# Memory attention and a top-1 expert layer on one core: the first batch reordered up to the choice of its expert, and a new table of places

## The chip, the core and the metric

The kernel runs on one core of one Trainium2 chip. The metric is the device time of one execution in microseconds (us). The core has five engines that each work through their own queue of instructions in order: PE (matmul; its weight loads are shown apart, as PEld), DVE (vector), ACT (scalar), POOL (general) and SP, which here issues every DMA. The engines wait for each other by semaphores. Sixteen DMA engines move data between HBM and the on-chip memory.

## What is computed

Eight batches, each with 8 heads, 576 tokens and head dimension 64. A softmax of `phi` over the tokens folds keys and values into 32 memory slots for each head; queries attend to these slots; each token's result (512 wide) goes to one of 8 experts, and the expert is chosen by token 0 and then kept or renewed token by token.

```python
a = phi - np.max(phi, axis=2, keepdims=True)
a = np.exp(a)
a = a / (np.sum(a, axis=2, keepdims=True) + 1e-09)
k_m = np.einsum('bhsm,bhsd->bhmd', a, k)
v_m = np.einsum('bhsm,bhsd->bhmd', a, v)
scores = scale * np.matmul(q, k_m.transpose(0, 1, 3, 2))
attn = softmax(scores)
x = np.matmul(attn, v_m)
logits = np.einsum('bsd,de->bse', x, w_gate)
fresh_e = int(np.argmax(logits[b, s]))
e = fresh_e if s == 0 or local_gate[b, s] < 0.5 else prev_e
h = np.maximum(x[b, s] @ w1[e], 0.0)
out[b, s] = p[e] * (h @ w2[e])
```

## The kernel before

**What runs for a batch.** For each batch there is, in this order: the softmax of phi (`colmax` the maximum over tokens, `pm`, `mc`, `pm2`, `cx` its way over partitions, `sub`, `exp`, `asum` the sum over tokens); `pkv`, 72 pairs of matmuls over nine groups of tokens that fold keys and values (tile `pkv`, L402); `sums` (L413), which brings the sums over tokens into the same PSUM tile; `rinv` and `kvn` (the division); `pT`, `kvT` (the turned form) and `pgg`, `ggt` (gate weights folded with the values). The attention is done in two parts of tokens, a (or p) and z: `qT` (queries turned on DVE), `psc` (scores, L513), `turn`, `mx`, `sub`, `exp`, `sum`, `inv`, `mul`, `at` (weights, L561), and `ah`, `al`, which split them into a high and a low half. `at store` writes them to DRAM.

**The choice.** `pl0` (L584) gives the eight logits of token 0 in tile `pl`. `c_choice` turns them on DVE into the expert's index `ei`; `expert` loads it into a register of SP; `w1 0`, `w1 1`, `w2 0`, `w2 1` then load that expert's weights into tiles `raw` (L761, L771).

**The expert.** `pg` and `G` fold w1 with the values (tiles `Gh`, `Gl`, high and low halves; L793, L805). The hidden layer (L825) runs in four chunks of 256 tokens and eight of 320, each with a PSUM tile `ph` of three in turn, which ACT and then DVE (tile `h`, L833 and L835) must empty. The second layer (tile `po`; L863 to L865 for the first tokens, L913 to L915 for the turned rest) uses w2 split into `w2h` (ACT, L782) and `w2l` (POOL, L783).

**What sets the order.** Everything is put into the engines' queues in the order in which the program is written. `start()` writes out by hand all work of batch 0 up to its first hidden chunk, mixed with the softmax of phi of batch 1. After it the generator `moe(b)` issues the hidden and the second layer of batch b and yields a modelled time after each chunk; the table `PLACES` gives for each step of each batch the modelled time (37.8 a batch) at which it is issued between these chunks. A step placed later stands behind more chunks in every queue that it uses. On SP, which also works in order, a load whose buffer isn't free yet holds up all loads behind it: behind w1 of batch 0 stand v of batch 1, w2, the next queries `q_t` (L253), phi, w2's second half, keys and values, and the store of `at`.

**Warm matmuls.** `warm(n)` issues n matmuls on zeros (tile `wp`, L305, 128 x 512) with no use for the result.

After the eight batches a loop over listed (batch, expert) pairs recomputes the tokens that left the expert of token 0; with these inputs it has no iteration.

## Time and profile before

| | |
|---|---|
| runs | 414.0, 413.4, 411.82 us; median 413.4 |
| the profiled execution | 414.21 us, its span 412.4 us |
| granted PE clock | 0.998 |
| PE busy | 391.7 us (95%), PEld 327.3 (79%) |
| DVE busy | 284.2 us (69%) |
| ACT, POOL busy | 179.4 us (44%), 151.3 us (37%) |
| DMA | 82.59 MB, mean 200 GB/s |

The span is what the profile's times are counted in; the profiled execution's own time is 1.8 us longer. PE stands still for 412.4 - 391.7 = 20.7 us in all, about 6 of them in the tail, where the last outputs are stored. Rows of a timeline read: start, length, engine, line, operation, out<-in, size, count, and in brackets the idle time before and what ended it. Rows of the chain read: start, length, engine or DMA, line. SPq is SP's work of issuing a DMA.

### The profile page before, as it was taken

The numbers are of one execution on the slowest core, as the hardware profiler recorded it, in microseconds if no ns is written. First come the engines' busy times: TensorE is split into PE (matmuls) and PEld (weight loads), VectorE is DVE, ScalarE is ACT, GpSimd is POOL, SyncE is SP. The second block draws the span as 40 slices with busy tenths as digits, with TensorE's granted clock in tenths as the row PEclk, the third lists the DMA queues.
The fourth block names the chain that finished last, engine by engine and source line by source line (L and its number), as shares of the span: only waits on it lengthen the run. The fifth ranks groups of instructions, "written<-read, shape, count | busy, mean of one in ns | idle before, by whom it ended". The sixth has DMA issues, their size and how long they took to land.

```text
span 412.4 us, 10572 instructions
## 1 busy us (share of the span) xinstructions
PE 391.7 (95%) x4170; PEld 327.3 (79%) x4174; DVE 284.2 (69%) x714; ACT 179.4 (44%) x434; POOL 151.3 (37%) x162
## 2 busy tenths in 40 slices
PE   8787888999999989999999999999999999999994
PEld 2546867898788967798878997799888996999883
DVE  5486797868977798697769777787767674736300
ACT  2153652446553744335542464445531563255010
POOL 3024451437341844029510691029400671065000
PEclk9999999999999999999999999999999999999999
DMA  8969792999297939699979197956784177002011
GB/s 238 328 201 269 139 396 95 232 255 383 61 357 160 369 106 241 140 351 351 263 169 399 28 282 146 338 227 175 159 209 170 31 238 288 28 0 65 25 39 57
DMA packets 115446, 82.59 MB, mean 200 GB/s; under 512 B 69616, under 2 KB 89088, under 8 KB 115392
## 3 DMA queue, kind: packets, MB, share of 16 engines
q1 hardware_dynamic: 115328, 81.84, 66.9%
q8 instruction: 35, 0.57, 0.6%
q0 software_dynamic: 64, 0.02, 0.2%
q14 instruction: 19, 0.16, 0.1%
HBM read 66.60 MB, written 15.24 MB: 198 GB/s over the span
## 4 chain that ended last, share of the span: by engine, by line
PE 68%; DMA 11%; SPq 11%; DVE 6%; issue 2%; ACT 1%; DVEq 0%; ACTq 0%
PE ph L825 19%; SPq L253 7%; PE po L863 7%; PE po L913 7%; PE po L865 6%; PE po L864 6%; PE po L915 6%; PE po L914 6%; DMA att_d<-at 6%; PE pkv L402 3%; PE pg L793 3%; DMA raw<-in_moe_w_dram 3%; DMA kv_t<-in_v_dram 2%; PE psc L513 2%; DVE h L835 1%
## 5 line engine op out<-in xcount | busy, mean ns | idle before, releaser
L783 POOL TENSOR_TENSOR w2l<-raw,w2h 128x512 fp32r<-128x512 f32 x64 | 82.4, 1312 | 29.3 <-ACT w2h L782 22.9
L825 PE MATMUL ph<-ah,Gh 128*128 128x256 f32 (+1 forms) x256 | 74.1, 304 | 2.1 <-DVE h L835 1.3
L835 DVE SCALAR_TENSOR_TENSOR h<-ph,h 128x320 fp32r<-128x320 f32 (+2 forms) x104 | 52.7, 519 | 32.2 <-ACT h L833 31.6
L825 PE MATMUL ph<-ah,Gl 128*128 128x256 f32 (+1 forms) x256 | 72.0, 296 | 0.1
L913 PE MATMUL po<-h,w2l 128*128 128x320 f32 x224 | 71.4, 319 | 0.0
L915 PE MATMUL po<-h,w2h 128*128 128x320 f32 x224 | 69.2, 309 | 0.0
L914 PE MATMUL po<-h,w2h 128*128 128x320 f32 x224 | 69.1, 309 | 0.0
L833 ACT ACTIVATE h<-ph 128x320 fp32r<-128x320 f32 (+1 forms) x96 | 46.4, 489 | 40.5 <-PE ph L825 40.2
L920 POOL TENSOR_TENSOR oT<-oT,gT 128x320 f32<-128x320 f32 x28 | 20.8, 742 | 107.5 <-DVE oT L919 93.7
L863 PE MATMUL po<-w2h,h 128*128 128x512 f32 (+1 forms) x152 | 60.0, 395 | 0.0
L864 PE MATMUL po<-w2l,h 128*128 128x512 f32 (+1 forms) x152 | 57.8, 380 | 0.5 <-POOL w2l L783 0.5
L865 PE MATMUL po<-w2h,h 128*128 128x512 f32 (+1 forms) x152 | 57.7, 380 | 0.0
L825 PE MATMUL ph<-al,Gh 128*128 128x256 f32 (+1 forms) x256 | 55.2, 296 | 0.5 <-issue 0.4
L825 PEld LDWEIGHTS ph<-ah,Gh 128*128 128x128 f32 x256 | 48.1, 188 | 7.4 <-DVE h L835 3.4
L825 PEld LDWEIGHTS ph<-ah,Gl 128*128 128x128 f32 x256 | 48.2, 188 | 0.5 <-DVE Gl L805 0.4
L913 PEld LDWEIGHTS po<-h,w2l 128*128 128x128 f32 x224 | 42.0, 188 | 5.0 <-issue 4.5
L569 POOL TENSOR_TENSOR al<-at,ah 128x576 fp32r<-128x576 f32 (+1 forms) x18 | 23.1, 1291 | 62.3 <-ACT ah L565 49.5
L782 ACT ACTIVATE w2h<-raw 128x512 fp32r<-128x512 f32 x64 | 38.4, 624 | 11.8 <-PE po L915 8.9
L914 PEld LDWEIGHTS po<-h,w2h 128*128 128x128 f32 x224 | 42.1, 188 | 0.2
L915 PEld LDWEIGHTS po<-h,w2h 128*128 128x128 f32 x224 | 42.1, 188 | 0.0
L825 PEld LDWEIGHTS ph<-al,Gh 128*128 128x128 f32 x256 | 41.2, 188 | 0.9 <-issue 0.6
L863 PEld LDWEIGHTS po<-w2h,h 128*128 128x128 f32 x152 | 28.6, 188 | 11.6 <-issue 7.0
(156 smaller groups left out, 581.4 us busy)
## 6 DMA issues: line engine op xcount, KB each, us to landing
raw<-in_moe_w_dram SPq DMA_DIRECT2D x34, 512.0 KB, 5.9
raw<-in_moe_w_dram SPq DMA_DIRECT2D x15, 1024.0 KB, 5.7
kv_t<-in_k_dram SPq DMA_DIRECT2D x7, 1152.0 KB, 10.0
kv_t<-in_v_dram SPq DMA_DIRECT2D x7, 1152.0 KB, 12.2
q_t<-in_q_dram SPq DMA_DIRECT2D x112, 72.0 KB, 3.4
att_d<-at SPq DMA_DIRECT2D x8, 576.0 KB, 7.6
out_dram<-oT SPq DMA_DIRECT2D x28, 160.0 KB, 5.8
out_dram<-ot SPq DMA_DIRECT2D x17, 256.0 KB, 5.4
```

Source lines behind the costliest of these rows:

```text
L253: nc.sync.dma_start(out=st.qt[p0 : p0 + 32, h], in_=qv[h, g, j])
L782: nc.scalar.activation(h, src, AF.Copy)
L783: nc.gpsimd.tensor_tensor(out=l, in0=src, in1=h, op=ALU.subtract)
L825: nc.tensor.matmul(pv[:, c - c0], lhsT=lt[:, g, cs], rhs=rt[:, g, s0 : s0 + n], start=(i == 0), stop=(i == 5),)
L833: nc.scalar.activation(hc[:, :, 0:n], pv, AF.Relu)
L835: nc.vector.scalar_tensor_tensor(out=hc[:, :, o : o + z - a], in0=pv[:, :, a:z], scalar=0.0, in1=hc[:, :, a:z], op0=ALU.max, op1=ALU.subtract,
L863: nc.tensor.matmul(po[:, c0:c1], lhsT=h[:, c, th], rhs=hi, start=(c == 0), stop=False)
L864: nc.tensor.matmul(po[:, c0:c1], lhsT=h[:, c, th], rhs=lo, start=False, stop=False)
L865: nc.tensor.matmul(po[:, c0:c1], lhsT=h[:, c, tl], rhs=hi, start=False, stop=(c == FC - 1))
L913: nc.tensor.matmul(po[:, 0:n], lhsT=lo, rhs=h[:, c, 0:n], start=(c == 0), stop=False)
L914: nc.tensor.matmul(po[:, 0:n], lhsT=hi, rhs=h[:, c, 0:n], start=False, stop=False)
L915: nc.tensor.matmul(po[:, 0:n], lhsT=hi, rhs=h[:, c, n : 2 * n], start=False, stop=(c == FC - 1))
```

## The change

The table of places gets new numbers. Keys and values are folded in two steps ("pkv 0" five groups of tokens, "pkv 1" four), the loads of queries are two steps ("q 0", "q 1"), and qT has two buffers. For batch 0 the sums come from one product with a block matrix of ones, in a PSUM tile of their own, ahead of the second piece of pkv, with rinv directly behind. The choice uses MAX and MAX_INDEX, and the index is loaded into SP's register without the two instructions that assert its bounds. `start()` is written in another order: 66 warm matmuls of 32 columns and 8 wide ones stand in place of 11 wide ones; the transposes of the larger part's queries stand ahead of `pl`, and nothing else; the choice stands ahead of `pm` of batch 1; the split of `at` into halves is done for each head group; exp and asum of batch 1 move out of `start()` into the table. In the first batch's loop "pg 1" and "pkv 0" stand between the first two hidden chunks. The scores of part z of batches 1 and 2 use PSUM tiles of the hidden layer, and `w_pg` takes another PSUM pool for the last batch's second half.

```diff
-    "pkv": {1: 1.52, 2: 34.49, 3: 70.3, 4: 93.6, 5: 127.71, 6: 165.81, 7: 204.5},
+    "pkv 0": {1: 0.14, 2: 30.71, 3: 66.71, 4: 92.5, 5: 127.8, 6: 165.6, 7: 203.7},
+    "pkv 1": {1: 1.86, 2: 32.7, 3: 66.71, 4: 94.32, 5: 127.8, 6: 165.6, 7: 203.7},
...
     def f_sums(st):
+        if st.b == 0:
+            st.sums = ps_a.tile([P, NG], F32, tag="pa", name="sums")
+            nc.tensor.matmul(st.sums, lhsT=st.asum.rearrange("p h m -> p (h m)"), rhs=ones, start=True, stop=True)
+            return
...
     def c_choice(st):
         pl = st.pl0
-        l0 = pga.tile([1, E], F32, tag="l0", name="l0")
-        m0 = pga.tile([1, 1], F32, tag="m0", name="m0")
+        m8 = pga.tile([1, 8], F32, tag="m8", name="m8")
         c0 = c0s[st.b % 2]
-        nc.vector.tensor_reduce(out=m0, in_=pl[0:1, 0:E], axis=AX.X, op=ALU.max)
-        nc.vector.scalar_tensor_tensor(
-            out=l0, in0=pl[0:1, 0:E], scalar=m0, in1=code[0:1], op0=ALU.is_equal, op1=ALU.mult
+        st.ei = pga.tile([1, 8], mybir.dt.uint32, tag="ei", name="ei", bufs=3)
+        nc.vector.max(out=m8, in_=pl[0:1, 0:E])
+        nc.vector.max_index(out=st.ei, in_max=m8, in_values=pl[0:1, 0:E])
+        nc.vector.tensor_scalar(
+            out=c0[0:1], in0=st.ei[:, 0:1], scalar1=-1.0, scalar2=float(E), op0=ALU.mult, op1=ALU.add
         )
-        nc.vector.tensor_reduce(out=c0[0:1], in_=l0, axis=AX.X, op=ALU.max)
-        st.ei = pga.tile([1, 1], I32, tag="ei", name="ei", bufs=3)
-        nc.vector.tensor_scalar(out=st.ei, in0=c0[0:1], scalar1=-1.0, scalar2=float(E), op0=ALU.mult, op1=ALU.add)
...
-        st.e = nc.sync.value_load(st.ei[0:1, 0:1], min_val=0, max_val=E - 1)
+        st.e = nc.values_load(
+            st.ei[0:1, 0:1],
+            engines=(mybir.EngineType.SP,),
+            min_val=0,
+            max_val=E - 1,
+            skip_runtime_bounds_check_because="an index of the gate's E values",
+        )
...
-        warm(11)
+        warm(66, 32)
+        warm(8)
...
-        warm(14)
+        warm(12)
...
         for i in range(2):
             f_asum_piece(s, i)
-            f_pkv(s, PIECES[i])
-            warm(3 * (1 - i))
+        f_pkv(s, PIECES[0])
         f_sums(s)
+        f_rinv(s)
+        warm(3)
+        f_pkv(s, PIECES[1])
         fetch_kv(n, (0,))
+        f_kvn(s)
         k_q0(s, EARLY[0])
-        f_rinv(s)
-        f_kvn(s)
+        f_pT(s)
+        warm(2)
+        f_kvT(s)
         f_colmax_tree(n, slice(0, 1))
-        warm(4)
-        f_pT(s)
-        warm(3)
-        f_kvT(s)
-        f_colmax_tree(n, slice(1, 4))
...
-        for f in steps:
+        for f in steps[:4]:
             f(s, EARLY[0])
-        p, z = EARLY[1:]
+        f_colmax_tree(n, slice(1, 2))
         k_q0(s, p)
-        f_pm(n)
-        warm(3)
-        f_mc(n)
+        for f in steps[4:]:
+            f(s, EARLY[0])
         c_pl(s)
+        f_colmax_tree(n, slice(2, 4))
         c_choice(s)
         expert(s)
```

On PE, at the start of batch 0, from the first pkv to the logits of token 0 (pq: transposed queries, wp: warm matmuls, of which only one of each stretch is shown). Before:

```order
L402 MATMUL pkv<-kv_t,phi_t 32x128 x48
...
L402 MATMUL pkv<-kv_t,phi_t 32x128 x24
L413 MATMUL pkv<-ones,asum 32x1 x8
L499 MATMUL pq<-ident,q0e 128x32 x4
...
L441 MATMUL pT<-ident,kvn 128x128 x2
...
L513 MATMUL psc<-qT,kvT 32x32 x8
L459 MATMUL pgg<-wg,kvT 32x9 x8
L502 MATMUL pq<-ident,q_147 64x128 x16
L346 MATMUL pm<-ident,cm 128x128
...
L584 MATMUL pl_399<-ggt_108,at 1x8 x2
```

The change, at the same place:

```order
L407 MATMUL pkv<-kv_t,phi_t 32x128 x48
L418 MATMUL sums<-ones,asum 128x2
...
L407 MATMUL pkv<-kv_t,phi_t 32x128 x24
L510 MATMUL pq<-ident,q0e 128x32 x4
L452 MATMUL pT<-ident,kvn 128x128 x2
...
L526 MATMUL psc<-qT,kvT 32x32 x8
L470 MATMUL pgg<-wg,kvT 32x9 x8
L513 MATMUL pq<-ident,q_149 64x128 x16
L597 MATMUL pl_439<-ggt_110,at 1x8 x2
L351 MATMUL pm<-ident,cm 128x128
```

The sums moved ahead of the second piece of pkv, pm of batch 1 moved behind pl, and pl stands directly behind the 16 transposes. Ahead of the first pkv stand 26 warm matmuls before and 87 in the change.

On PE, in batch 0's hidden layer, from the end of the first chunk to the third (pg: w1's second half folded with the values; pkv: batch 1's; only the first row of a chunk is shown). Before:

```order
L793 MATMUL pg<-raw_421,kvT 32x512 x8
L825 MATMUL ph<-ah,Gh 128x256
...
L402 MATMUL pkv<-kv_t,phi_t 32x128 x72
L413 MATMUL pkv<-ones,asum 32x1 x8
L825 MATMUL ph<-ah,Gh 128x256
```

The change:

```order
L805 MATMUL pg<-raw_455,kvT 32x512 x8
L407 MATMUL pkv<-kv_t,phi_t 32x128 x40
L838 MATMUL ph<-ah,Gh 128x256
...
L407 MATMUL pkv<-kv_t,phi_t 32x128 x32
L422 MATMUL pkv<-ones,asum 32x1 x8
L838 MATMUL ph<-ah,Gh 128x256
```

40 of the 72 pairs moved ahead of the second chunk; the other 32 and the sums stay between the second and the third.

On DVE, in batch 2's hidden layer, around the column maximum of batch 4 (cm; sc: scores of the attention; qT: turned queries; h: hidden chunks of 256 and then 320 tokens). Before:

```order
L835 SCALAR_TENSOR_TENSOR h_2152<-ph,h_2152 128x2x256
L486 STREAM_TRANSPOSE qT<-q_t 128x576
L835 SCALAR_TENSOR_TENSOR h_2152<-ph,h_2152 128x2x256
L310 TENSOR_REDUCE cm<-phi_t 128x128
L835 SCALAR_TENSOR_TENSOR h_2255<-ph,h_2255 128x320
L549 TENSOR_REDUCE sm<-sc 128x18
```

The change:

```order
L848 SCALAR_TENSOR_TENSOR h_2183<-ph,h_2183 128x2x256
L315 TENSOR_REDUCE cm<-phi_t 128x128
L848 SCALAR_TENSOR_TENSOR h_2183<-ph,h_2183 128x2x256
L848 SCALAR_TENSOR_TENSOR h_2284<-ph,h_2284 128x320
L562 TENSOR_REDUCE sm<-sc 128x18
```

The column maximum moved ahead of the last chunk of 256 tokens, and a transpose of queries left this stretch. Elsewhere, `pl` of batch 1 stands behind 14 po rows of three matmuls in the change and behind 12 before, and pl of batch 6 moved from the end of batch 4's second layer into batch 5's hidden layer.

## The prediction

> **What bounds the kernel now.** I read the busy shares first, then the busy time stage by stage, then PE's waits, then the chain of work that ended last. The stages (start, rest of batch 0, then 46 us for each batch) show where PE has anything left to win. The first number behind the window is its length, the second PE's busy time; the last three are PE's granted clock, the DMA share and GB/s:

> ```profile
> 0.00:29.61 29.61, 23.13 (x380) 12.65 (x384) 17.35 (x46) 10.10 (x23) 4.73 (x30) 1.00 0.84 252
> 29.61:80.00 50.39, 44.73 (x495) 35.99 (x488) 39.79 (x93) 22.91 (x57) 22.83 (x28) 1.00 0.84 236
> 80.00:126.00 46.00, 46.00 (x503) 39.18 (x502) 38.88 (x107) 23.84 (x60) 19.35 (x16) 1.00 0.82 245
> 126.00:172.00 46.00, 44.67 (x654) 35.46 (x652) 37.25 (x90) 23.37 (x57) 19.10 (x15) 1.00 0.74 206
> ```

> PE is idle 29.61 - 23.13 = 6.48 us before the first hidden matmul of batch 0 and 50.39 - 44.73 = 5.66 us in the rest of that batch, then 0 and 1.33 us in two whole batches, at a full clock. From 80 us on the kernel is PE's own work in PE's own order. A new table of places that keeps this work can only take idle time away, so the change is worth what it does in the first 80 us and to a few single waits later. Idle time ahead of 29 us counts only where it lies on the chain that ends in the chosen expert's weights. That chain (start, length, what):

> ```profile
> 11.14 1.58 PE pkv L402 x95
> ...
> 17.00 1.39 issue
> ...
> 18.79 1.90 PE pq L502 x32
> ...
> 21.60 0.19 PE pl L584 x4
> ...
> 21.81 0.17 DVE m L597
> ...
> 22.57 0.14 DVE ei L603
> ...
> 23.27 0.18 SPq L1046
> ...
> 23.75 0.41 SPq L761
> ...
> 51.29 12.46 DMA att_d<-at
> ```

> The load of v ends, then pkv, psc and the transposes of the queries (pq) follow; the logits of token 0 (pl) choose the expert, and at 23.75 SP issues the load of w1. Behind it SP issues v of batch 1, w2, the next queries, the next keys and values and the store of at, so everything that the DMAs carry from 24 to 64 us hangs on 23.75.

> **The start, part by part.**

> ```profile
> 1.19 4.21 PE L305 MATMUL wp<-wz 128*128 128x512 bf16 x11 [1.19 <-DVE wz L163]
> L305 PEld LDWEIGHTS <-wz 128*128 128x128 bf16 x43 | 4.3, 109 | 6.9 <-issue 3.5 <-DVE wz L163 1.2
> 10.79 0.29 DVE L393 TENSOR_TENSOR asum<-asum,tree 128x128 f32<-128x128 f32 x1
> 15.11 0.37 ACT L433 ACTIVATE kvn<-pkv,rinv 128x128 f32<-128x128 f32 x1
> ```

> The sums of batch 0 become one matmul ahead of the second piece of pkv, and rinv follows while PE works on. So kvn, which began at 15.11 behind pkv, sums and rinv, starts straight behind pkv, which ended near 14.4: 0.7 us earlier, 0.5 with seams. Of the warm matmuls behind it, two go from in front of pT and one from behind it.

> The 66 small warm matmuls ahead of everything have no row. A pkv pair takes 1.58 / 95 = 0.017 us, and a weight load of a warm matmul 0.109, so all take between 1.1 and 7.2 us. I take 0.05 each, 3.3 us, since their 32 columns stand nearer to pkv. With the eight wide ones (8/11 of 4.21 = 3.1) the first pm is issued at 7.6, where the eleven ended at 5.4. What hides it is v, on which pkv waits until 11.14: asum ended at 11.08 and sums need it only when pkv 0 is through, at 12.7. asum 2.2 us later, at 13.3, would hold sums for 0.6; but from here to the gate there are 1.4 us of slack, as follows. I take 0. At 7.2 us asum would come at 17.2 and the slack would be gone.

> The 1.39 us "issue" stall stands inside psc, among matmuls of one kind with their inputs there.

> ```profile
> 0.00:17.10 17.10, 13.79 (x218) 6.90 (x221) 8.16 (x19) 3.69 (x7) 3.47 (x28) 1.00 0.95 273
> 17.10:41.80 24.70, 19.16 (x379) 13.42 (x380) 17.29 (x43) 11.89 (x27) 7.97 (x10) 1.00 0.81 243
> ```

> From this stall to the next one of its kind (42.07, quoted below) lie 379 matmuls and 380 weight loads, 759 instructions, near to three times 256: I read both as instructions that are loaded by the block and came late while the DMAs were full. Ahead of the first pkv now stand 61 more warm matmuls with their weight loads (87 against 26), 122 instructions, so both this boundary and the one a block before it come earlier: the one before moves out of pkv into the warm matmuls that run while v is awaited, and the next block is asked for some microseconds sooner. So the stall leaves the chain. [...]

> Then PE meets the queries. The larger part's transposes now stand ahead of pl. Their loads, by issue and landing:

> ```profile
> L291 SPq DMA_DIRECT2D q<-in_q_dram x2: 1574/2163/2752, 6.8 to 9.5; - x2
> DMA to landing us min/median/max: 8.8/8.9/9.1
> ```

> The second is issued at 9.5 and lands 8.8 later, at 18.3. The transposes take the two head groups in turn, one from each load, so the 1.9 us cannot run before, and pl comes at 20.3 to 20.45. I take 20.45, against 21.60: 1.15 us. Upstream, 0.5 and 1.39 make 1.9; the softmax of the small part, about 2.5 us on DVE, then ends near 19, ahead of pl by 1.4. That is the slack: what is won upstream beyond it is lost here.

> The choice takes 0.90 us from m to the end of ei (21.81 to 22.71). MAX and MAX_INDEX have no row: four operations with their gaps make 0.90, so two make 0.45, and 1.0 if the index costs three. I take 0.5: 0.4 us won. SP's assert instructions behind the register load (from 23.27 to just ahead of 23.58) go: 0.26. So w1 is issued 1.15 + 0.4 + 0.26 = 1.8 us earlier, at 21.95. The ends: -1.7 (sums at 17.2 in place of 12.7, so pl 3.1 later, and the dear index 0.5) and 2.1 (pl at 20.3, an index as cheap as m).

> How much of this lead reaches PE is decided further on:

> ```profile
> 33.03 1.09 PE L793 MATMUL pg<-raw,kvT 64*32 64x512 f32 x16 [0.97 <-DMA raw<-in_moe_w_dram]
> 36.05 2.25 PE L402 MATMUL pkv<-kv_t,phi_t 64*32 64x128 f32 x144 [0.31 <-DMA kv_t<-in_v_dram]
> 39.12 0.39 PE L825 MATMUL ph<-ah,Gh 128*128 128x256 f32 x1 [0.78 <-DVE Gl L805]
> 42.07 0.39 PE L825 MATMUL ph<-al,Gh 128*128 128x256 f32 x1 [0.43 <-issue]
> ```

> Before: chunk 0, pg 1, chunk 1, pkv, sums, chunk 2 (39.12). Now pkv 0, five of nine tokens, stands between pg 1 and chunk 1, and queued behind it are chunk 1, pkv 1, sums and chunk 2, with ACT and DVE waiting for their results. pkv 0 needs v, which landed at 36.0; 1.8 us earlier that is 34.2, while pg 1 is through at 34.12 - 1.8 = 32.3. So PE idles 1.9 us there, then runs pkv 0 (5/9 of 2.25 = 1.25), chunk 1 (36.05 - 0.31 - 34.12 = 1.6), pkv 1 (1.0) and sums (0.25): chunk 2 at 34.2 + 4.1 = 38.3, a gain of 0.8, which is SP's lead less 1.0. Gl's 0.78 lies under the new order, as G 1 has some 5 us. Of the 0.43 I count 0.3, since its block boundary moves too. Start together: **-1.1**.

> **The places.**

> ```profile
> 60.12 0.50 PE L864 MATMUL po<-w2l,h 128*128 128x512 f32 x1 [0.46 <-POOL w2l L783]
> 64.80 0.24 PE L584 MATMUL pl<-ggt,at 128*1 128x8 f32 x4 [1.20 <-DVE at L561]
> 276.99 0.24 PE L584 MATMUL pl<-ggt,at 128*1 128x8 f32 x4 [0.59 <-DVE at L561]
> 55.11 0.69 PE L513 MATMUL psc<-qT,kvT 64*32 64x288 f32 x8 [0.59 <-DVE qT L486]
> ```

> pl of batch 1 moves behind six more po matmuls (some 1.4 us of work), which cover its 1.20, and the cause, the store of at (51.29, 12.46 us), goes out earlier with all that is ahead of it on SP: **-1.2**, at worst 0. pl of batch 6 moves by several chunks: **-0.6**. w2's second load has SP's lead of 1.8 against PE's of 1.1: **-0.3** of 0.46. psc of batch 1 waits for qT, which now stands behind one more h on DVE (0.48 below): **+0.4**.

> The fourth wait is 1.33 us. The column maximum of batch 4's phi sits on DVE between two h, and PE needs the h behind it to free one of three buffers:

> ```profile
> 141.52 0.69 DVE L835 SCALAR_TENSOR_TENSOR h<-ph,h 128x512 fp32r<-128x512 f32 x1
> 143.56 2.24 DVE L310 TENSOR_REDUCE cm<-phi_t 128x128 f32<-128x1152 f32 x1
> 145.72 0.48 DVE L835 SCALAR_TENSOR_TENSOR h<-ph,h 128x320 fp32r<-128x320 f32 x1
> 146.25 0.41 PE L825 MATMUL ph<-ah,Gh 128*128 128x320 f32 x1 [1.33 <-DVE h L835]
> ```

> It moves ahead by one h. Then it runs from 142.2 to 144.4, the h behind it (0.69) ends near 145.05, and that one frees the buffer of the chunk one earlier, which was due 0.9 us ahead of the stalled one (146.25 - 1.33 - 0.9, about 143.95): a wait of 1.1. The 2.24 us are moved, not hidden: **-0.2**, though -1.33 if DVE is early for another reason.

> New waits: some hundred entries moved, and the whole batches above had between none and 1.33 us. I allow one of the middle size, **+0.6**. The second query buffer, pkv in two pieces and pg 1 in another pool add no work; I cost them at nothing, hidden under PE's own work as the full stage above is, and at one wait of 1.3 if that cover is gone.

> Sum: -1.1 - 1.2 - 0.6 - 0.3 + 0.4 - 0.2 + 0.6 = -2.4 us. The profiled execution took 414.2 (span 412.4), 0.8 above the median of 413.4 and at the top of 411.8 to 414.0. The sum gives 411.8 against 414.2 and 411.0 against the median; I predict 411.0.

> **Rivals.** *The gains are absorbed*: pkv 0 eats the lead, the store of at lands when it did (12.46 us in a stage with a DMA share of 0.84), and PE waits as before, somewhere else. Only -0.6 and -0.3 stay: 413.3, or 412.5 from the median. For it: both first stages are full on DMA. *All targeted waits go*: a lead of 2.1 (-1.1 and -0.43), then 1.2, 0.59, 0.46, 0.59 and 1.33, and no new wait: -5.7, so 408.5, or 407.7 from the median. Against it: qT behind one more h, and the 2.24 us that only move. *On the other side, the small warm matmuls hold up asum*, the gate, and with it v, and pkv 0 stands ahead of chunk 1. Slower from where the lead is under 1.0: pl past 21.25, sums past 14.9, asum 3.8 late, which is 0.075 us for each of the 66. At 0.109, pl is 3.1 later, the lead 1.85 - 3.1 = -1.25, and chunk 2 comes 2.25 later; w2's saving is lost: 414.2 + 2.25 - 1.2 - 0.6 + 0.4 + 0.6 = 415.65, and 416.15 with the dear index. Against it: pkv's narrow products at 0.017. *The change doesn't do what it says*: the stall comes back between pkv and pl. It costs up to 1.39, as much as the slack there, so the forecast stands.

> **How the numbers follow.** A measurement of this kernel tells about 0.5%, 2.07 us, from no change: the bounds are 411.3 and 415.5. The forecast (409.5 to 412.3) has 0.50, six parts in ten of it below 411.3. Absorbed: 0.22. All waits gone: 0.18. Slower by the warm matmuls: 0.10, most of it past 415.5. Faster is 0.30 + 0.18 and a little of the absorbed, 0.51; slower 0.08; the same 0.41. The range takes in the absorbed case, the forecast and most of "all waits gone", and stops short of the slower case: 407.4 to 414.8.

> **What would show it.** Right: w1 issued near 22.0; no issue stall between pkv and pl; pl at 20.4 straight behind the transposes; a new wait of PE for v of 1.5 to 2 us ahead of pkv 0; chunk 2 near 38.3; no wait of pl for at in batches 1 and 6; a wait of about 1 us left at the column maximum of batch 4. Wrong: a lead of SP under 1.0, sums waiting for asum, or waits of over 0.6 us in batches that had none.

## The result and the profile after

The change takes 415.8 us (median of nine runs, 414.17 to 417.8) against 412.63 (nine runs of the kernel before, 411.63 to 414.14). The ratio is 1.0078, with a 95% interval of 1.0052 to 1.0103: slower by 0.8%, where 411.0 was predicted and 414.8 was the end of the range. The profiled execution took 415.16 us (span 413.4, PE clock 0.986). The profiled execution of before that the prediction used was a long one: a second profile of the same kernel (e8 below) took 412.15, and its 2.0 us lie behind the third hidden chunk of batch 0, half of them ahead of batch 1. One execution of e4, of 954 us, is left out of every time below.

The stages of the change, in the columns used before (length, busy time of PE, PEld, DVE, ACT and POOL, clock, DMA share, GB/s):

```profile
0.00:29.61 29.61, 22.58 (x377) 13.95 (x378) 14.70 (x40) 7.86 (x18) 4.58 (x31) 0.94 0.79 234
29.61:80.00 50.39, 43.60 (x488) 35.10 (x487) 38.72 (x94) 22.66 (x59) 20.38 (x19) 0.97 0.77 238
80.00:126.00 46.00, 45.80 (x510) 38.59 (x509) 39.22 (x94) 24.71 (x61) 20.85 (x25) 1.00 0.78 241
126.00:172.00 46.00, 44.81 (x652) 36.60 (x658) 37.46 (x92) 22.40 (x57) 20.24 (x17) 1.00 0.81 218
```

PE is idle for 7.03 us in the first stage (6.48 before) and 6.79 in the second (5.66), and the clock, 1.00 in both before, is 0.94 and 0.97: nearly all of the loss is ahead of 80 us, and part of it is busy time at a lower clock, which a sum of idle times doesn't show. PE's waits over the whole execution (in total, times, longest) name the places:

```profile
PE pkv L407 <- issue: 6.1, 3, 3.4
PE psc L526 <- DVE qT L497: 1.9, 1, 1.9
PE pkv L407 <- DMA kv_t<-in_v_dram: 1.8, 1, 1.8
PE ph L838 <- DVE h L848: 1.2, 2, 1.0
```

No wait of pl for at, of po for w2l or of ph for Gl is left over 0.2 us: the targeted waits have gone. In their place stand three waits of pkv that the profile puts down to nothing ("issue") and one of psc for qT. The timeline of PE has the start of it (start, length, instruction, count, and in brackets the idle time ahead):

```profile
1.19 5.20 PE L310 MATMUL wp<-wz 128*128 128x32 bf16 x74 [1.19 <-DVE wz L167]
...
11.83 1.58 PE L407 MATMUL pkv<-kv_t,phi_t 64*32 64x128 f32 x96 [1.81 <-DMA kv_t<-in_v_dram]
...
14.32 0.65 PE L407 MATMUL pkv<-kv_t,phi_t 64*32 64x128 f32 x28
18.37 0.63 PE L407 MATMUL pkv<-kv_t,phi_t 64*32 64x128 f32 x20 [3.40 <-issue]
...
21.05 2.98 PE L513 MATMUL pq<-ident,q 128*64 128x128 f32 x32
23.96 0.24 PE L597 MATMUL pl<-ggt,at 128*1 128x8 f32 x4
```

PE stops 28 matmuls into the second piece of pkv, with 20 matmuls of the same kind and the same operands left, and resumes at 18.37. Before, it stopped inside psc and resumed at 18.39. The stall did not leave the chain: it became 2 us longer, ended at the same time, and has more work behind it. That work also runs slower: the granted clock is 0.50 from 19.74 to 23.15, and on the chain the 32 transposes take 2.90 us where they took 1.90. pl ends at 24.20, not at the 20.4 predicted. From there DVE's choice and SP's issue follow:

```profile
24.24 0.16 DVE L610 MAX8 m<-pl 1x8 f32<-1x8 f32 x1 [0.31 <-PE pl L597]
24.44 0.08 DVE L611 MATCH_VALUE_LOAD ei<-m,pl 1x8 f32 x1
24.51 0.15 DVE L611 FIND_INDEX8 ei<-m,pl 1x8 uint32<-1x8 f32 x1
```

```profile
25.38 1.56 SPq L772 DMA_DIRECT2D raw<-in_moe_w_dram  x3
```

From the end of pl (L597) to the first load of w1 it is 25.38 - 24.20 = 1.2 us; before, 23.75 - 21.79 = 2.0. The choice won its 0.8 and w1 still goes out 1.6 us later than before (predicted: 1.8 earlier). Two more rows of PE's timeline and the load of v of batch 1 show what this lateness does in the first hidden chunks:

```profile
37.83 1.47 PE L407 MATMUL pkv<-kv_t,phi_t 64*32 64x128 f32 x80 [1.84 <-issue]
...
42.75 0.33 PE L407 MATMUL pkv<-kv_t,phi_t 64*32 64x128 f32 x6 [0.83 <-issue]
...
59.93 0.69 PE L526 MATMUL psc<-qT,kvT 64*32 64x288 f32 x8 [1.95 <-DVE qT L497]
```

```profile
L235 SPq DMA_DIRECT2D kv_t<-in_v_dram x1: 498/498/498, 27.0 to 27.0; - x1
...
DMA to landing us min/median/max: 10.8/10.8/10.8
```

The 1.84 ahead of pkv 0 is the wait for v, though the profile names no releaser: v is issued at 27.0 and lands 10.8 later, at 37.8, where pkv 0 starts. It was predicted as 1.9. The 0.83 stands inside pkv 1 with all operands there, and 1.95 stands where the prediction had 1.0 (0.59 + 0.4).

To see where a kernel gains or loses, I compared the start of the first hidden matmul of each batch, and of the last po. Worked out from the traces; us later (+) or earlier (-) than in the profile of before that the prediction used:

```
                 before   change     e1      e2      e3      e4      e8
batch 0           29.61    +2.11   -2.50   -0.77   +6.41   +3.42   +0.34
its third chunk   39.12    +4.04   -0.25   +1.64   +6.48   +6.16   +0.06
batch 1           88.30    +4.46   +0.18   +2.08   +7.83   +6.55   -0.98
batch 2          135.60    +4.92   +4.34   +2.54   +9.25   +6.65   -0.97
batch 3          186.38    +3.27   +3.58   +1.37  +12.06   +6.28   -1.75
batch 5          279.90    +0.70   +7.44   -0.33  +11.71   +6.11   -1.98
last po          406.05    +0.59   +8.71   -0.43  +11.71   +6.31   -2.00
```

The change loses 4.5 us by the first hidden chunk of batch 1 and wins 3.9 of them back by the end; against e8, the more usual execution of before, the two are 5.4 lost and 2.9 won.

### The profile page after: what moved, and what is told of

Its sections match the earlier page's. It is cut to its first block, busy times and chain, and to the rows that moved or that the text cites. A ratio compares the mean times of both kernels' runs of the same rounds, so it can differ in the third digit from the quotient of the medians.

```text
span 413.4 us, 10639 instructions
## 1 busy us (share of the span) xinstructions
PE 391.7 (95%) x4216; PEld 331.6 (80%) x4216; DVE 284.6 (69%) x714; ACT 177.9 (43%) x435; POOL 151.2 (37%) x164
## 4 chain that ended last, share of the span: by engine, by line
PE 87%; DMA 4%; DVE 3%; issue 2%; ACT 1%; SPq 1%; POOL 0%; DVEq 0%
PE ph L838 23%; PE po L926 9%; PE po L876 8%; PE po L928 8%; PE po L927 8%; PE po L877 8%; PE po L878 8%; PE pkv L407 4%; PE pg L805 4%; PE psc L526 2%; DMA kv_t<-in_v_dram 2%; DMA kv_t<-in_k_dram 2%; PE pl L621 1%; PE pq L513 1%; PE po L900 1%
## 5 line engine op out<-in xcount | busy, mean ns | idle before, releaser
L793 ACT ACTIVATE w2h<-raw 128x512 fp32r<-128x512 f32 x64 | 38.4, 623 | 9.0 <-PE po L928 9.0
```

What stands on the lines that cost most here:

```text
L793: nc.scalar.activation(h, src, AF.Copy)
```

## The experiments

Two theories were tried first. **A**: PE's instructions come in blocks; a block that PE reaches before it has been loaded stops it; the number of instructions ahead of the first pkv decides where such a boundary falls, and the change moved it into pkv. **B**: the stop comes from the new order of the start (sums early, rinv, the split pkv), or from the DMAs, wherever the boundaries are. Unless said otherwise, each experiment is the change with the edit shown.

**e1: the old warm matmuls in the new order** (126 instructions fewer).

```diff
-        warm(66, 32)
-        warm(8)
+        warm(11)
```

> The change with the head of before: 11 wide warm matmuls in place of 66 narrow and 8 wide ones, so 126 instructions fewer stand ahead of the first pkv and all else is the change. Theory A (a block of PE's instructions arrives late): in the change the 3.40 us stall stands at the 29th matmul of pkv's second piece because a block of 256 ends there; the boundary moves 126 instructions on, past the rest of pkv, the transposes and psc, to the first transposes of the larger part's queries, which wait for q until 18.3 to 19 anyway. No issue stall in pkv; kvn before 15; w1 issued between 22 and 23.3 (25.38 in the change); first hidden matmul near 29; time 410.5 to 412.5. Theory B (the second piece of pkv waits for something of the new order itself, v or the sums, that the profile names issue): the stall of 3 to 3.5 us stays in pkv's second piece, time 415 to 417. Theory C (the table of places is what costs): start earlier or not, time over 414.

Measured: 422.46 us (four runs), ratio 1.0230 [1.0166, 1.0295]. The start came out as A has it, with the stop gone from pkv and batch 0's hidden layer 2.5 us ahead of before. The time was missed by 10 us: four stops of 1.2 to 2.9 us without a releaser came back in later batches. PE's timeline at batch 2's sums and the po behind them:

```profile
128.55 0.16 PE L422 MATMUL pkv<-ones,asum 64*32 64x1 f32 x1 [2.02 <-issue]
...
129.07 0.47 PE L927 MATMUL po<-h,w2h 128*128 128x320 f32 x1
...
132.15 0.31 PE L927 MATMUL po<-h,w2h 128*128 128x320 f32 x1
```

So 126 instructions fewer moved the later stops as well, not the first alone. And this stop of 2.0 us costs more than 2.0: the next eleven po start 0.27 us apart, where later ones start 0.15 apart, at a granted clock of 0.50, so that is another 1.3 us.

**e2: 32 narrow warm matmuls more**, 64 instructions, a quarter of a block.

```diff
-        warm(66, 32)
+        warm(98, 32)
```

> The change with 98 narrow warm matmuls in place of 66: 64 instructions more ahead of the first pkv. Theory A: the boundary that stood in pkv's second piece moves to sums, at about 13.4, and the one a block before it moves from the first pkv (11.8) into the warm matmuls at about 6, so the next block is asked for some 5 us sooner and is there when PE needs it: no stall over 1 us in pkv, sums or psc; w1 issued 22 to 23.3; time 410.5 to 412.5. If the block's loading takes the DMA queue's time whatever it stands behind, it still arrives near 18.4 and PE stalls at sums for 4 to 5 us: time 416.5 to 418.5. Theory B: the stall stays in the second piece of pkv, time 415 to 417. The 32 more narrow ones take about 1 us, so pm is issued 1 us later, which v covers by all theories.

Measured: 413.16 us, 1.0015 [0.9985, 1.0045]; it does more work than the change and takes 2.6 us less, though more than the 410.5 to 412.5 that were expected. PE's timeline:

```profile
14.93 0.94 PE L407 MATMUL pkv<-kv_t,phi_t 64*32 64x128 f32 x48
...
18.25 1.97 PE L513 MATMUL pq<-ident,q 128*64 128x128 f32 x32 [0.36 <-DMA q<-in_q_dram]
20.27 0.37 PE L597 MATMUL pl<-ggt,at 128*1 128x8 f32 x4
...
37.35 0.63 PE L407 MATMUL pkv<-kv_t,phi_t 64*32 64x128 f32 x21
39.90 0.78 PE L407 MATMUL pkv<-kv_t,phi_t 64*32 64x128 f32 x38 [1.92 <-issue]
```

All 48 run through, the transposes wait for q as the prediction had it, pl is at 20.27 (predicted 20.45), and w1 goes out at 21.81 (21.95). The next boundary now stops PE in pkv 1 of batch 1, for 1.92 us.

**e3: the change's head in the kernel before.**

```diff
-        warm(11)
+        warm(66, 32)
+        warm(8)
```

> The kernel before with the head of the change (66 narrow and 8 wide warm matmuls for 11 wide ones) and nothing else. Theory A: before's stall of 1.39 us at the 13th psc matmul moves 126 instructions forward into pkv's second piece, where it lasts 3 to 4.5 us, since it ends at about 18.4 as in both kernels; kvn near 19, pl near 23.5 to 24.5 (21.60), w1 issued near 25.5 to 26.5; time 414.5 to 416.5. Theory B: no stall in pkv, since the order of sums and pkv is the old one; time within 1 us of before.

Measured: 423.86 us, 1.0249 [1.0210, 1.0288]. In the old order and with the old table PE stops in pkv as well (PE's timeline):

```profile
1.19 1.94 PE L305 MATMUL wp<-wz 128*128 128x32 bf16 x66 [1.19 <-DVE wz L163]
...
14.49 0.66 PE L402 MATMUL pkv<-kv_t,phi_t 64*32 64x128 f32 x28
18.64 0.85 PE L402 MATMUL pkv<-kv_t,phi_t 64*32 64x128 f32 x18 [3.50 <-issue]
```

This ends B: the order of the start isn't needed for the stop, the count alone brings it. The time, expected at 414.5 to 416.5, was missed by 7 us. It also gives the small warm matmuls their price, 1.94 / 66 = 0.029 us. At the first hidden matmul 6.4 us are lost, more than the stop, and the granted clock is 0.50 for 6.8 us behind it. By batch 3 it is 12.1 us, with three more stops of this kind on the way (0.9, 0.8 and 1.9 us) and a wait of 1.7 of psc for qT.

**e4: the old places.** Everything that the table issues after 37.8 (behind batch 0's loop) goes back to where it was, with the PSUM pools that hang on it. A line of many:

```diff
-    "pgg": {1: 9.9, 2: 44.79, 3: 73.1, 4: 97.61, 5: 135.78, 6: 172.1, 7: 210.8},
+    "pgg": {1: 9.9, 2: 39.5, 3: 73.1, 4: 100.59, 5: 138.8, 6: 176, 7: 213.8},
```

> The change with before's places for everything that is issued after batch 0's own work (the new places for batch 0, for batch 1's phi and keys and for the steps ahead of 37.8 stay), and with the PSUM pools of before for pg 1 and the scores of batch 2. By the traces the change gained 3.9 us between the first hidden matmul of batch 1 and the end, 1.2 of it in waits of PE and the rest where small steps stand side by side. If the table did that, this one takes 418 to 420. If the gain came from the second query buffer or from the later start itself (loads that land earlier relative to PE), it takes 415 to 416.5.

Measured: 419.37 us (three runs), 1.0134 [1.0093, 1.0175], against 1.0078 for the change. From batch 1 to the end it wins 0.2 us, where the change wins 3.9: the new table is worth about 0.5% by the times (the intervals overlap) and 3.6 us by the two traces. That is the upper end. The other runs with the new table (e2, e5, e6, e7, e9, e10 and e12) win 1.8 to 2.6 us in the same stretch, and e8, before itself, wins 1.0 there, which the long execution lost.

Next came the other terms, each with the stop taken out of pkv (90 narrow matmuls).

**e5: 90 narrow matmuls, e6: with pkv 0 behind the second chunk, e7: with qT where it was, e8: before again** (a blank line taken out, for a second profile).

```diff
-        warm(66, 32)
+        warm(90, 32)
```

e6 and e7 add one line each:

```diff
-    "pkv 0": {1: 0.14,
+    "pkv 0": {1: 1.86,
```

```diff
-    "a qT 1": {1: 11.4,
+    "a qT 1": {1: 10.7,
```

> The change with 90 narrow warm matmuls in place of 66 (98 still met a late block at 37.7, the 21st matmul of batch 1's second piece of pkv, for 1.92 us, and one of 0.6 later). Theory A, blocks of 256 asked for when PE enters the block before, and there about 6.5 us later in the first 60 us: at 90 the boundary of 37.7 moves 16 instructions on, to the end of that pkv, and the next ones leave the small steps too; no issue stall over 1 us behind pkv of batch 0, start of chunk 2 between 38.5 and 39.5, time 409.5 to 412, under before. Rival: the waits for v ahead of pkv 0 (1.8 to 2.4 us, called issue in part) and for qT (1.9) and the clock behind them are what is left of the loss: chunk 2 still at 40 or later, 412.5 to 415.

> As the one with 90, and batch 1's pkv 0 is issued behind the second hidden chunk, directly ahead of pkv 1, as pkv stood before. By the prediction's step (SP's lead less 1.0) PE's wait of about 2 us for v ahead of pkv 0 is covered by 1.4 us of chunk 1, so chunk 2 comes 1 to 1.4 us sooner than with 90 alone, and the time is 0.8 to 1.5 us less. Rival: v and the late block end the wait at the same time whatever stands ahead, and the boundary then stands inside 144 narrow products in a row: chunk 2 within 0.5 us, time the same or up to 2 us more.

> As the one with 90, and the second transpose of batch 1's queries (a qT 1) is issued one chunk sooner, at its old place. The prediction gave its move +0.4: PE's wait for qT at psc (1.95 us in the change, 0.59 before) falls by 0.4 to 0.5, time less by as much. Rival: the wait is set by DVE's chain of small steps and by the step pr, which took 1.27 us there in the change and 0.17 before, and qT's place does nothing: time the same.

> The kernel before, unchanged but for one blank line, for a second profile: whether its 1.39 us issue stall in psc, the end of that stall near 18.4, and the 0.17 us of DVE's first step pr come again. Theory A: the stall comes again at the same matmul within 2 of it and ends between 18 and 19. Rival: these are chance of one execution, and the stalls of another stand elsewhere.

Measured: e5 413.09, 1.0026 [1.0004, 1.0049]; e6 411.36, 0.9982 [0.9956, 1.0007]; e7 411.23, 0.9997 [0.9967, 1.0027]; e8 411.61, 0.9996 [0.9969, 1.0023]. In e5 the rival came true: no late block stops PE by more than 0.6 us, and the waits for v ahead of pkv 0 (2.19) and for qT (1.94) are left. With pkv 0 behind the second chunk e6 is some 0.4% faster than e5, though their intervals just touch, and by the traces it takes 10.3 us from the first hidden matmul to the third chunk, e5 11.7; this although in e6 a late block stands where the wait for v was (PE's timeline):

```profile
33.86 1.79 PE L407 MATMUL pkv<-kv_t,phi_t 64*32 64x128 f32 x110
37.84 0.73 PE L407 MATMUL pkv<-kv_t,phi_t 64*32 64x128 f32 x33 [2.18 <-issue]
```

e7's qT brings the wait of psc from 1.95 to 1.54 us, the 0.4 that the prediction gave that move. Its time is below e5's by more than that, but the intervals overlap. e8's stop is at the matmul where the profile of before has it (PE's timeline):

```profile
17.31 0.39 PE L512 MATMUL psc<-qT,kvT 64*32 64x32 f32 x13
18.43 0.25 PE L512 MATMUL psc<-qT,kvT 64*32 64x32 f32 x3 [0.74 <-issue]
```

The place is the same in both executions; the length (0.74 here, 1.39 in the first profile) is not.

**e9: the three edits together (with 86), e10: and the fifth split of w2 later.** In e7 1.54 us of psc's wait were left. On DVE, `pr` held the engine for 1.27 us ahead of qT, while POOL's w2l was running; before, pr took 0.17 us and w2l began 0.57 us behind it. e10 moves that split:

```diff
-    "split 4": {0: 11.6,
+    "split 4": {0: 12.9,
```

> The change with 86 narrow warm matmuls, pkv 0 of batch 1 behind the second chunk, and its second queries' transpose at the old place. If the loss of the change is the late blocks, the wait for v that pkv 0 puts ahead of chunk 1, and qT: with 86 the boundary in pkv's row of 144 products (2.2 us of stall with 90) moves 8 instructions on, still inside it, so 1.5 to 2.5 us of stall stay there or it falls to under 1; chunk 2 near 38.5; psc's wait for qT 1.5; time 409.5 to 411, ratio to before 0.994 to 0.998. [...]

> As the one before, and the first split of w2's second half in batch 0 is issued one chunk later, so that POOL's w2l starts behind DVE's step pr and not 0.03 us ahead of it. If that start is what holds pr for 1.27 us in place of 0.17, pr takes 0.17 again, PE's wait for qT at psc falls from 1.5 to between 0.3 and 0.6 us, and the time by 1 to 2.5 us (the clock stays up as well): 408 to 410. Rival: pr's 1.27 has another cause, and stays; time the same as the one before, within 0.5.

Measured: e9 410.41, 0.9964 [0.9939, 0.9990]; e10 409.96, 0.9932 [0.9905, 0.9959], a version that beats both kernels. pr on DVE, w2l on POOL and psc on PE, in their timelines, first of the change and then of e10:

```profile
57.12 1.27 DVE L721 TENSOR_TENSOR pr<-pe,es 32x18 f32<-32x18 f32 x1
...
57.09 4.96 POOL L794 TENSOR_TENSOR w2l<-raw,w2h 128x512 fp32r<-128x512 f32 x4 [7.03 <-ACT w2h L793]
```

```profile
56.72 0.17 DVE L721 TENSOR_TENSOR pr<-pe,es 32x18 f32<-32x18 f32 x1
...
57.00 3.76 POOL L794 TENSOR_TENSOR w2l<-raw,w2h 128x512 fp32r<-128x512 f32 x3 [6.23 <-ACT w2h L793]
...
58.03 0.69 PE L526 MATMUL psc<-qT,kvT 64*32 64x288 f32 x8 [0.43 <-DVE qT L497]
```

With w2l 0.11 us behind pr's end instead of 0.03 us ahead of its start, pr is back at 0.17 and the wait of psc falls from 1.5 to 0.43. The time of e10 over that of e9 is within the intervals; 1 to 2.5 us less had been expected. In e3 and e11, with before's table, w2l also began just ahead of pr (0.08 and 0.04 us), and pr took 1.28 and 1.26: pr was long in these where w2l began first, and not by the new table.

**e11: the choice alone in the kernel before.** MAX and MAX_INDEX, and the index loaded without the asserts (the same edit as in the diff of the change).

> The kernel before with the change's choice alone (MAX, MAX_INDEX, the register load without the two assert instructions); PE's instructions and the table stay. The change's trace has 1.16 us from the end of pl to the issue of w1, before had 1.96: w1 is issued 0.7 to 0.8 sooner, at about 23, first hidden matmul 0.5 to 0.8 sooner, and the time 0.3 to 0.8 less: 411.0 to 411.5 against 411.7. Rival: the store of at and the queries absorb it: time the same within 0.2.

Measured: 412.24, 0.9985 [0.9957, 1.0013]. From the end of pl to w1 it is 1.2 us, 0.8 less than before, and the time cannot be told from before's. In its trace w2l begins ahead of pr, and psc waits 1.7 us for qT (0.59 before), so the lead may be lost there; whether 0.8 us of it is worth anything by itself stays open.

**e12: 128 narrow matmuls more than the change**, 256 instructions.

```diff
-        warm(66, 32)
+        warm(194, 32)
```

> The change with 194 narrow warm matmuls: 128 more than the change's 66, with their weight loads 256 instructions, one whole block. If blocks of 256 are what stalls PE, every boundary falls where it falls in the change: PE stops again at the 29th matmul of pkv's second piece (28 done, 20 left), although 98 narrow ones (64 instructions on) had no stop there. The 128 take 3.7 us at the 0.029 that they cost in the change, so pm, asum and pkv come up to 3 us later and the stop may be shorter, 1.5 to 3.5 us; time 416 to 420. Rival (the stop depends on how much stands ahead, not on the place within a block): no stop there, or another matmul.

Measured: 416.16, 1.0118 [1.0082, 1.0153]. PE's timeline:

```profile
14.37 0.66 PE L407 MATMUL pkv<-kv_t,phi_t 64*32 64x128 f32 x28
18.35 0.63 PE L407 MATMUL pkv<-kv_t,phi_t 64*32 64x128 f32 x20 [3.32 <-issue]
```

With a quarter of a block more (e2) the stop leaves pkv; with a whole block more it is back at the same matmul, after 28 of 48, at the same time and nearly the same length. So the place of the stop goes by the count of instructions, with a period of 256. A period of 64 is out by e2, one of 128 by e1, which has 126 instructions fewer and no stop there.

That it is instructions which come late can be read from the list of DMA queues, where one is named instruction (queue, packets, MB, share of 16 engines). The page of the change, and that of e12:

```profile
q8 instruction: 35, 0.57, 0.6%
```

```profile
q8 instruction: 36, 0.59, 0.7%
```

256 instructions more are one packet more, and e1, with 126 fewer, has 34. Worked out from the traces, the packet of q8 ahead of a stop and the time at which PE goes on:

```
                  packet of q8      PE goes on   idle time, us
before, psc       15.83 to 17.03      18.39           1.39
e8, psc           15.76 to 16.95      18.43           0.74
e11, psc          16.39 to 17.58      19.10           1.11
change, pkv       15.73 to 16.92      18.37           3.40
e3, pkv           16.17 to 17.38      18.64           3.50
e12, pkv          15.64 to 16.79      18.35           3.32
change, pkv 1     39.81 to 41.39      42.75           0.83
e2, pkv 1         37.16 to 38.59      39.90           1.92
e6, pkv           34.89 to 36.56      37.84           2.18
```

PE goes on 1.3 to 1.6 us behind the end of the packet in all nine. Leaving aside the waits for v ahead of pkv 0, the 14 traces have 22 idle times of PE of over 0.6 us that the profile calls issue. All 22 end 1.2 to 1.6 us behind a packet; the waits for v do not, they end where v lands (37.8 in the change).

## Why the prediction was wrong

**The step that failed** is this one: "the one before moves out of pkv into the warm matmuls that run while v is awaited, and the next block is asked for some microseconds sooner. So the stall leaves the chain." That it is a block of 256 that came late was right (e3, e12 and the packets of q8): the prediction had only one distance of 759 instructions for it, and e12 measured the period of 256. That 122 more instructions take it off the chain was only an argument from the direction in which the boundary moves. Where it lands was not worked out, though the trace of before had all that it takes: ahead of the stop stood 218 matmuls and 221 weight loads. PE's work in the change up to its stop:

```profile
0.00:15.00 15.00, 11.80 (x221) 6.42 (x221) 6.19 (x12) 2.82 (x4) 3.59 (x30) 1.00 0.87 258
```

The place in the program is the same, 221 for 218. With 92 matmuls of these instead of 31 ahead of the first pkv, some 128 are left behind it: 96 of the first piece, 2 sums, 3 warm ones, and 28 of the second piece. And what sets the end of the stop was missed. PE goes on at 18.37 or 18.39 whether it comes there at 15 or at 17. In the trace of before the packet begins at 15.83, while PE still works until 17.00, so it is asked for ahead of the stop. What asks for it is not shown; I took it to be PE's entry into the block before, 128 matmuls earlier, which is an estimate from the count. In the change that is the first pkv (11.83), in before about the sixtieth (12.1), so by this estimate the next block was not asked for "some microseconds sooner" but 0.3 us. In the seven traces that stop here PE goes on 5.6 to 6.8 us behind that entry, and in the change it had run through these 256 instructions in 3.1 us (11.83 to 14.97). What sets the time from the entry to the packet is not shown either: it is 2.9 to 4.3 us in these seven, with the DMA queue q1 at 109.8% in the change (15.70 to 16.95):

```profile
q1 hardware_dynamic: 713, 0.35, 109.8%
q8 instruction: 1, 0.02, 6.0%
```

In the change, with the boundary earlier but the entry still behind the wait for v, the stop is only longer (3.40 for 1.39). By the count the entry missed the last of the warm matmuls by one or two; with 32 more, in e2, it lies among them, ahead of that wait, the packet begins at 5.80, and pkv has no stop here.

**The rival "the change doesn't do what it says"** had the right event and the wrong price: "it costs up to 1.39, as much as the slack there, so the forecast stands." It cost 3.40, and 1.0 more in the transposes at the low clock behind it; the slack of 1.4 was gone at once, and nothing bounded the stall by its old length. With the change's own lead of -1.6 in place of 1.8, the working gives for chunk 2 about 39.12 + 1.0 + 1.6 = 41.7, and 42.5 with the 0.83; the trace has 43.2, and the 0.7 between them I have not placed.

The other steps, by the runs:

- The start without the stop: right. In e2 pl at 20.27 and w1 at 21.81, for 20.45 and 21.95.
- The small warm matmuls: 0.029 each for 0.05, so the slower rival's mechanism (they hold up asum) didn't occur: asum was ready at 11.4, ahead of the sums at 13.3. The slower side was reached in another way.
- The choice: 0.4 + 0.26 predicted, 0.8 measured, also in e11.
- pkv 0 waits for v, 1.9 predicted: 1.84, right; by e6 this order costs some 0.4%.
- The 0.43 stall, of which 0.3 was counted as won: wrong, it became 0.83, and 1.92 in e2. It is the same kind of boundary, and e12 has it at the same matmul as the change.
- pl of batches 1 and 6, w2l, Gl: all four waits gone, as predicted. In the change PE also came later by 4 us, which makes that no test; in e6, where it comes 0.2 to 0.5 earlier than before, they are gone as well.
- psc of batch 1: 0.59 + 0.4 predicted, 1.95 measured. The 0.4 was right (e7). The rest, 1.0, is pr behind POOL's w2l (e10), which the prediction had not seen. After this wait eight po start 0.43 us apart instead of 0.23, 1.6 us more.
- The column maximum of batch 4: a wait of 1.1 predicted, 1.01 measured.
- The table behind batch 1: -0.6 - 0.2 + 0.6 predicted, no new wait and -3.9 measured, 1.8 to 2.6 in the other runs with this table: a term mis-sized. The idle time isn't where most of it lies. PE from the first hidden matmul of batch 3 to that of batch 7, in the windows of before and of the change:

```profile
186.38:367.75 181.37, 180.35 (x1818) 156.29 (x1817) 127.61 (x319) 82.68 (x200) 72.69 (x63) 1.00 0.66 197
```

```profile
189.65:368.24 178.59, 178.59 (x1818) 156.43 (x1817) 126.98 (x318) 81.78 (x200) 72.03 (x62) 1.00 0.68 195
```

The same 1818 matmuls take 1.0 us less idle time and 1.8 us less busy time, at the same clock. By the count of the trace the small steps (all but ph and po) stand among the hidden and second layers in 27 groups instead of 31 over these four batches; 1.8 / 4 is some 0.44 us for each group saved. That it is the seams is read from the trace and wasn't tried by itself. The sentence "A new table of places that keeps this work can only take idle time away" was too strong.

Put together against e8, the change is 5.4 us behind at batch 1, by the stop and what followed it, the wait for psc and the low clock, and wins 2.9 back behind it.

## What to carry to other kernels

Where PE stops between two instructions of one kind with all operands there, count its instructions to the next such stop, and look whether a packet of the instruction queue ends just ahead of both. If the count is near a multiple of 256, as here (759 in before, near three times 256, and 256 in e12), the program's length ahead of it is part of the tuning, and any edit that adds or removes instructions (a warm-up, a split step) moves the later stops, as in e1 and e2. Try some paddings a quarter of a block apart before an edit is judged: here one and the same order went from 1.0230 (e1) to 1.0015 (e2) by warm matmuls alone. And a stall is priced by what ends it and by where it lands, not by the length it had: work out both before it is counted as gone.

## What the runs showed of the hardware

```profile
63.16 0.63 PE L876 MATMUL po<-w2h,h 128*128 128x512 f32 x1
63.58 0.63 PE L877 MATMUL po<-w2l,h 128*128 128x512 f32 x1
...
64.30 0.40 PE L876 MATMUL po<-w2h,h 128*128 128x512 f32 x1
64.53 0.40 PE L877 MATMUL po<-w2l,h 128*128 128x512 f32 x1
```

- **DVE behind POOL.** A DVE operation on 32 x 18 elements took 1.27 us instead of 0.17 when a POOL operation on 128 x 512 had begun 0.03 us ahead of it. Where the POOL operation began behind its end, by 0.11 us in e10 and 0.57 in before, it took 0.17. What makes it long is not shown.
